# Attention in a three-stage kernel: the product with V from split float32r, batch by batch, to plain float32, both batches in column halves of one product

## The chip, the cores and the metric

The kernel runs on one core of a Trainium2 chip. The metric is the device time of one launch in microseconds (us). TensorE (PE) does the matrix products, and its weight loads are listed apart as PEld. VectorE is DVE, ScalarE is ACT, GpSimd is POOL, and SP issues most DMAs. TensorE and the transposes write to PSUM, and DVE or ACT move the results from there to SBUF.

## The reference, cut to what matters

```python
# attention: B, H, S, D = 4, 8, 576, 64
scores = scale * np.matmul(q, k.transpose(0, 1, 3, 2))
...
scores = scores + bias.transpose(2, 0, 1)[None, :, :, :]   # bias: a small MLP of the relative position
scores = scores - np.max(scores, axis=-1, keepdims=True)
attn = np.exp(scores)
attn = attn / (np.sum(attn, axis=-1, keepdims=True) + 1e-09)
return np.matmul(attn, v).astype(np.float32)
...
x = np.ascontiguousarray(attn_out.transpose(0, 2, 1, 3)).reshape(B * S, H * D)
x = _moe_ref(x=x, **moe_kwargs)          # router logits x @ w_gate, top expert of 8, two layers
return _moe2_ref(x=x, **moe2_kwargs)     # dense 512 -> 2048 -> 512
```

## The kernel before

The launch runs four phases one after the other: the position bias (`bias_phase`, to 78 us in the trace), attention (to 380 us), the experts (`moe1`) and the dense layers (`moe2`). Most products use the type float32r: a value is split into an upper part that float32r holds exactly and a lower rest, and three or two products of parts stand for one float32 product.

Attention goes through 32 units. A unit is (p, g, h): a pair p of batches (0 and 1, or 2 and 3), a group g of query rows (g = 0: rows 0 to 255, g = 1: rows 256 to 575) and a head h. The order is p, then g, then h, so there are four groups of eight units: (p, g) = (0,0), (0,1), (1,0), (1,1). A unit of g = 0 has four tiles of 128 query rows, two for each batch. One of g = 1 has five: the first takes 64 rows of either batch (`b` is None), then two for each batch.

Tile s goes through these stages, in steps of a software pipeline that is written out by hand, since PE, DVE, ACT and SP keep the order in which the code is written:

- step s: `stage_s` (scores, L429, into a PSUM tile `s` with two buffers), `stage_softmax` (L440 on DVE adds the bias and takes the row minimum of the negated scores, and a read of the accumulator follows), and late in the step `stage_exp` (L450 on ACT, with the row sum by an accumulator read).
- step s + 2: `stage_t` and `stage_r` transpose the 576 columns in four pieces of 128 (L463) and one of 64 (L473). `stage_hi` copies the upper part to `eh` on ACT (L487, L481; the 64-row rest L486, L479), and `stage_lo` subtracts on DVE to get the lower part `el` (L494, L507; the rest L499, L503).
- `AVL` = 4 steps after the last tile of a batch: `stage_av`, nine products (five with `eh` at L525, four with `el` at L527) whose weights are `vs`: V's upper part in 64 columns and its lower part in 64 more. `stage_oevac` copies the sums to `ot` on ACT (L538). So each unit has two such steps.
- one step later: `stage_j` (L549) multiplies `ot` by `jw`, 64 columns of identity (which adds the two parts of V) and 8 of the router's weights, and `stage_x` (L578, DVE) divides by the row sums into `xrow`. In g = 1 the 64-row rest has two more small products, L552 and L554, in the two column halves of TensorE's array.

`o` and `jp` share one PSUM buffer (`ps_v`). The scores' PSUM tile has two, so the scores of tile s + 2 wait until the exp of tile s has read its buffer:

```python
self.ps_s = eb.enter_context(tc.tile_pool(name="ps_s", bufs=2, space=PSUM))
self.ps_v = eb.enter_context(tc.tile_pool(name="ps_v", bufs=1, space=PSUM))
```

`load_kv` brings K and V of one batch and head into a raw buffer, and `prep_kv` splits both into `ks` and `vs`: casts on DVE or ACT (L321, L326, L324), subtractions on POOL (L322, L327). Twelve of the 32 are split in the bias phase, the rest within attention (`KVJ`, `KVR`, `KVA`), most of those of the second pair in group (0,1). Routing work of finished groups is fed in between, an operation or so a step (`slip`). At the end, `moe1` has the first expert's weights loaded by POOL into four buffers `stg`, whose space attention used before.

Of the kernel before, what the change touches and what calls it, by code (L numbers as in the profile page):

```python
# [120 lines left out]
def host_arrays(i):  # L121
# [21 lines left out]
    jw = np.zeros((2, 64, H, 72), np.float32)  # L143
    wg = i["moe_w_gate"].reshape(H, D, E).transpose(1, 0, 2)
    jw[:, :, :, 0:64] = np.eye(64, dtype=np.float32)[None, :, None, :]
    jw[:, :, :, 64:72] = wg[None]
    a["jw"] = jw.reshape(128, H, 72)
# [17 lines left out]
class Kernel:  # L165
# [4 lines left out]
    def bias_phase(self, prep_hook):  # L170
        nc, tc, a = self.nc, self.tc, self.a
        with ExitStack() as es:
# [11 lines left out]
            self.raw += [xp.tile([128, S + 5 * D], F32, name=f"kv{j}") for j in range(NRAW - 2)]  # L184
# [108 lines left out]
            PREP = 770.0 * KV0 / 26  # L293
# [12 lines left out]
    def load_kv(self, b, h):  # L306
        nc, a = self.nc, self.a
        bh = b * H + h
        buf = self.raw[self.nkv % len(self.raw)]
        self.nkv += 1  # L310
        kr, vr = buf[0:64, 0:S], buf[:, S:S + 5 * D].rearrange("p (c d) -> p c d", c=5)
# [4 lines left out]
    def prep_kv(self, b, h, veng):  # L316
        nc = self.nc
        kr, vr = self.kvraw.pop((b, h))
        vs = self.kv_p.tile([128, 5, 2 * D], F32R, tag="vs", name="vs")
# [56 lines left out]
    def attention(self):  # L376
# [4 lines left out]
        for u in units:  # L381
# [5 lines left out]
            for j, (bb, t) in enumerate(ts):  # L387
                tiles.append(dict(u=u, b=bb, t=t, c=4 if bb is None else 2 * bb + t, j=j, first=(j == 0), last=(j == len(ts) - 1),
                                  end=(bb is not None and t == 1)))
        n = len(tiles)  # L390
# [4 lines left out]
        def unit_state(u):  # L395
            if u not in st:
# [4 lines left out]
                d["eh"] = self.et_p.tile([128, 2, 5, 320], F32R, tag="eh", name="eh")  # L401
                d["el"] = self.et_p.tile([128, 2, 4, 320], F32R, tag="el", name="el")
                for bb in range(2):
                    d["eh", bb], d["el", bb] = d["eh"][:, 1 - bb], d["el"][:, 1 - bb]
# [70 lines left out]
        def stage_hi(i):  # L475
            T = tiles[i]
            d = st[T["u"]]
            if T["b"] is None:
                nc.scalar.activation(out=d["eh"][0:64, :, 4, 0:64], in_=d["rem", None].rearrange("p (b q) -> p b q", b=2),  # L479
                                     func=AF.Copy)  # L480
# [90 lines left out]
        def stage_x(i):  # L571
# [9 lines left out]
            if T["last"]:  # L581
# [9 lines left out]
                if h == H - 1:  # L591
                    self.routed.append((p, g))
# [1064 lines left out]
```

## Time and profile before

| | us |
|---|---|
| runs | 1093.06, 1093.54, 1095.12; median 1093.54 |
| the profiled execution | 1093.54, of which the span is 1091.9 |
| bias phase | to 78.06 |
| attention, group (0,0) / (0,1) / (1,0) | 58.67 / 90.88 / 64.81 |
| attention, group (1,1), to the end of its last full unit of work | 82.30 |
| from there to the end | 717 |

The groups are cut where the first L440 of a group starts, the last one 10.2 us after its last unit's first L440. "Busy" counts the time in which at least one instruction of an engine runs. Instructions of one engine overlap by some 0.08 us on DVE and ACT and by far more on PE, so the distance between starts, not the listed duration, is what an instruction costs its engine.

### The profile page before, as it was taken

The numbers are of one execution on the slowest core, as the hardware profiler recorded it, in microseconds if no ns is written. First come the engines' busy times: TensorE is split into PE (matmuls) and PEld (weight loads), VectorE is DVE, ScalarE is ACT, GpSimd is POOL, SyncE is SP. The second block draws the span as 40 slices with busy tenths as digits, with TensorE's granted clock in tenths as the row PEclk, the third lists the DMA queues.
The fourth block names the chain that finished last, engine by engine and source line by source line (L and its number), as shares of the span: only waits on it lengthen the run. The fifth ranks groups of instructions, "written<-read, shape, count | busy, mean of one in ns | idle before, by whom it ended". The sixth has DMA issues, their size and how long they took to land. (4 is left out here: it accounts for less than half of the span.)

```text
span 1091.9 us, 19524 instructions
## 1 busy us (share of the span) xinstructions
PE 1035.2 (95%) x6878; PEld 906.6 (83%) x6878; DVE 702.0 (64%) x1438; ACT 551.5 (51%) x1163; POOL 276.7 (25%) x437
## 2 busy tenths in 40 slices
PE   9999998999999989899899999999999999999996
PEld 3349988889998878777787888998989989899895
DVE  7779989989999895887887712533525335253350
ACT  7779877778787733444545513432424224242240
POOL 5646536665335343111211200000000000000000
PEclk9999999999999989999999999999999999999999
DMA  9985585764656477896744824600010100100000
GB/s 230 313 249 172 157 213 154 200 163 147 191 139 173 136 161 242 251 266 211 244 164 134 280 68 165 248 36 30 11 39 3 38 30 11 39 1 20 10 11 20
DMA packets 94566, 146.58 MB, mean 134 GB/s; under 512 B 11264, under 2 KB 53328, under 8 KB 94352
## 3 DMA queue, kind: packets, MB, share of 16 engines
q1 hardware_dynamic: 88976, 127.26, 39.8%
q0 software_dynamic: 5456, 17.70, 5.3%
q8 instruction: 64, 1.05, 0.4%
q14 instruction: 70, 0.57, 0.2%
HBM read 105.36 MB, written 36.70 MB: 130 GB/s over the span
## 5 line engine op out<-in xcount | busy, mean ns | idle before, releaser
L1415 PE MATMUL l1x<-xTl,wih 128*128 128x256 f32 x576 | 163.0, 283 | 0.0
L1415 PE MATMUL l1x<-xTh,wil 128*128 128x256 f32 x576 | 163.0, 283 | 0.0
L1415 PE MATMUL l1x<-xTh,wih 128*128 128x256 f32 x576 | 163.0, 283 | 0.0
L1423 DVE SCALAR_TENSOR_TENSOR t<-e,t 128x512 f32<-128x512 f32 x72 | 49.8, 692 | 132.8 <-ACT t L1422 132.8
L450 ACT ACTIVATE e<-s,mn 128x576 f32<-128x576 f32 x144 | 106.1, 737 | 33.1 <-DVE mn L440 26.8
L1439 POOL DMA_INDIRECT out<-y,idc x18 | 17.6, 979 | 395.2 <-ACT xTh L1404 271.3
L440 DVE CUSTOM_DVE_ANT_0 s<-s,bt 128x576 f32<-128x576 f32 x144 | 108.7, 755 | 7.3 <-PE s L429 4.3
L1434 PE MATMUL l2x<-woh,gTh 128*128 128x512 f32 x288 | 112.8, 392 | 0.0
L1434 PE MATMUL l2x<-wol,gTh 128*128 128x512 f32 x288 | 112.3, 390 | 0.0
L1434 PE MATMUL l2x<-woh,gTl 128*128 128x512 f32 x288 | 112.1, 389 | 0.0
L1415 PEld LDWEIGHTS l1x<-xTl,wih 128*128 128x128 f32 x576 | 110.6, 192 | 0.4
L1415 PEld LDWEIGHTS l1x<-xTh,wih 128*128 128x128 f32 x576 | 110.6, 192 | 0.4
L1415 PEld LDWEIGHTS l1x<-xTh,wil 128*128 128x128 f32 x576 | 110.6, 192 | 0.0
L1426 ACT ACTIVATE gTh<-t 128x512 fp32r<-128x512 f32 x72 | 45.5, 632 | 111.9 <-DVE t L1424 111.9
L429 PE MATMUL s<-ks,qh 128*128 128x288 f32 x320 | 92.7, 320 | 4.5 <-ACT e L450 4.4
L494 DVE TENSOR_TENSOR el<-t,eh 128x512 fp32r<-128x512 f32 x128 | 87.4, 683 | 2.8 <-DMA xgat<-in_kT 0.7
L463 PE MATMUL t<-ident,e 128*128 128x128 f32 x576 | 86.8, 273 | 0.5 <-DVE el L494 0.5
L1438 ACT ACTIVATE y<-l2x 128x512 f32<-128x512 f32 x18 | 10.8, 598 | 142.6 <-PE l2x L1434 142.6
L1427 DVE TENSOR_TENSOR gTl<-t,gTh 128x512 fp32r<-128x512 f32 x72 | 49.8, 692 | 50.4 <-ACT gTh L1426 50.4
L1188 PE MATMUL l2m<-w2h,hTl 128*128 128x512 f32 x168 | 69.9, 416 | 10.1 <-DVE hTl L1147 10.1
L487 ACT ACTIVATE eh<-t 128x512 fp32r<-128x512 f32 x128 | 75.2, 588 | 5.8 <-PE t L463 4.2
L1188 PE MATMUL l2m<-w2h,hTh 128*128 128x512 f32 x168 | 70.5, 419 | 5.8 <-ACT hTh L1146 5.6
(248 smaller groups left out, 2510.5 us busy)
## 6 DMA issues: line engine op xcount, KB each, us to landing
bt<-bias SPq DMA_DIRECT2D x32, 576.0 KB, 5.0
stg<-in_moe_w SPq DMA_DIRECT2D x32, 512.0 KB, 4.2
dec_w<-in_w SPq DMA_DIRECT2D x32, 512.0 KB, 5.4
bias<-o SPq DMA_DIRECT2D x36, 295.5 KB, 5.0
x_d<-y SPq DMA_DIRECT2D x22, 260.0 KB, 4.1
qraw<-in_qT SPq DMA_DIRECT2D x32, 160.0 KB, 3.7
k<-ks SPq DMA_DIRECT2D x32, 144.0 KB, 4.2
bt<-bias SPq DMA_DIRECT2D x32, 144.0 KB, 5.9
```

The costliest lines, as they stand in the source:

```text
L429: nc.tensor.matmul(out=ps[:, half, 0:288], lhsT=x, rhs=k[:, half * 288:half * 288 + 288], start=(m == 0), stop=(m == len(seq) - 1))
L440: nc.vector.tensor_tensor_reduce(out=sc, in0=sc, in1=bt[:, t, :].rearrange("p (a k) -> p a k", a=2), scale=-0.125, scalar=3.0e38, op0=ALU. ...
L450: nc.scalar.activation(out=e.rearrange("p (a k) -> p a k", a=2), in_=T["ps"][:, :, 0:288], func=AF.Exp, scale=-1.0, bias=T["mn"], accum_ou ...
L463: nc.tensor.transpose(out=tp[:, c, :], in_=e[:, 128 * c:128 * c + 128], identity=ident)
L487: nc.scalar.activation(out=d["eh", T["b"]][:, 0:4, o:o + 128], in_=T["tp"], func=AF.Copy)
L494: nc.vector.tensor_tensor(out=d["el", bb][:, 0:4, o:o + n_], in0=src, in1=d["eh", bb][:, 0:4, o:o + n_].bitcast(F32), op=ALU.subtract)
L1188: nc.tensor.matmul(out=p, lhsT=hT[h][:, k, 128 * t:128 * t + 128], rhs=w2[wt][:, k, :], start=(k == 0 and h == wt), stop=(k == 7 and wt == 1))
L1415: nc.tensor.matmul(out=p[:, m, :], lhsT=wi[wt][:, k, ms], rhs=xT[x][:, k, :], start=(n == 0), stop=(n == 11))
L1423: V.scalar_tensor_tensor(out=t, in0=e, scalar=1.0, in1=t, op0=ALU.add, op1=ALU.mult)
L1426: nc.scalar.activation(out=gT[0][:, gs, :], in_=t, func=AF.Copy)
L1427: V.tensor_tensor(out=gT[1][:, gs, :], in0=t, in1=gT[0][:, gs, :].bitcast(F32), op=ALU.subtract)
L1434: nc.tensor.matmul(out=p, lhsT=gT[h][:, k, 128 * t:128 * t + 128], rhs=wo[wt][:, k, :], start=(n == 0), stop=(n == 47))
```

## The change

V is no longer split: `load_kv` brings it straight into `vs` (plain float32, 20 buffers), and `prep_kv` handles K alone. The transposed weights are not split either: `stage_hi` and `stage_lo` become `stage_e`, one copy to a float32 tile `et`, on ACT for the four big pieces and on DVE for the 64-row rest. The two `et` tiles are fixed, used by units in turn, and rows 64 to 127 of their fifth piece are set to zero once. `stage_av` runs once a unit, four steps after its last tile: five pieces, each with one product for either batch in its own column half (64 weights columns, `tile_position`), in plain float32. `stage_oevac` is one copy on DVE instead of two on ACT. `stage_j` has two products of 144 columns instead of four of 72, since `jw` now has a block for each half, and `stage_x` is one operation a unit. Special orders for the last tiles (`late`, `tail_psum`) are gone. `PREP`, the load that the bias phase's planner books on DVE for the preparation of K and V, falls from 770 to 350 per unit of it.

```diff
-    jw = np.zeros((2, 64, H, 72), np.float32)
+    jw = np.zeros((2, 64, H, 2, 72), np.float32)
...
-            PREP = 770.0 * KV0 / 26
+            PREP = 350.0 * KV0 / 26
...
+        vs = self.kv_p.tile([128, 5, D], F32, tag="vs", name="vs", bufs=20)
         nc.sync.dma_start(out=kr, in_=a["kT"][bh])
-        nc.sync.dma_start(out=vr, in_=a["v"][bh])
-        self.kvraw[b, h] = (kr, vr)
...
+        nc.sync.dma_start(out=vs, in_=a["v"][bh])
+        self.kvraw[b, h] = (kr, vs)
...
-        if veng == "a":
-            nc.scalar.activation(out=vs[:, :, 0:D], in_=vr, func=AF.Copy)
-        else:
-            nc.vector.tensor_copy(out=vs[:, :, 0:D], in_=vr)
-        nc.gpsimd.tensor_tensor(out=vs[:, :, D:2 * D], in0=vr, in1=vs[:, :, 0:D].bitcast(F32), op=ALU.subtract)
...
+        for j in range(2):
+            et = self.et_p.tile([128, 2, 5, 320], F32, name=f"et{j}")
+            nc.gpsimd.memset(et[64:128, :, 4, :], 0.0)
+            ets.append(et)
...
-            if T["end"]:
-                nc.scalar.activation(out=d["eh", T["b"]][0:64, 4, o - 128:o + 128], in_=d["rem", T["b"]], func=AF.Copy)
-            nc.scalar.activation(out=d["eh", T["b"]][:, 0:4, o:o + 128], in_=T["tp"], func=AF.Copy)
-
-        def stage_lo(i):
+            if T["end"]:
+                nc.vector.tensor_copy(out=d["et", T["b"]][0:64, 4, o - 128:o + 128], in_=d["rem", T["b"]])
+            nc.scalar.activation(out=d["et", T["b"]][:, 0:4, o:o + 128], in_=T["tp"], func=AF.Copy)
+
+        def stage_av(i):
...
             for c in range(5):
-                nc.tensor.matmul(out=o[:, :N], lhsT=vs[:, c, :], rhs=eh[:, c, :N], start=(c == 0), stop=False)
-            for c in range(4):
-                nc.tensor.matmul(out=o[:, :N], lhsT=vs[:, c, :], rhs=el[:, c, :N], start=False, stop=(c == 3))
+                for bb in range(2):
+                    nc.tensor.matmul(out=o[64 * bb:64 * bb + 64, :N], lhsT=self.kv[2 * p + bb, h][1][:, c, :],
+                                     rhs=d["et", bb][:, c, :N], start=(c == 0), stop=(c == 4),
+                                     tile_position=(0, 64 * bb))
             T["o"] = o
...
+            d["ot"] = self.o_p.tile([128, 320], F32, tag="ot", name="ot")
+            nc.vector.tensor_copy(out=d["ot"][:, :N], in_=T["o"][:, :N])
...
+            jp = ps_v.tile([128, 5, 72], F32, tag="v", name="jp")
             for t in range(2):
-                nc.tensor.matmul(out=jp[:, t, :], lhsT=d["ot", bb][:, o0 + 128 * t:o0 + 128 * t + 128],
-                                 rhs=jw[:, h, :], start=True, stop=True)
...
+                nc.tensor.matmul(out=jp[:, t:4:2, :], lhsT=d["ot"][:, o0 + 128 * t:o0 + 128 * t + 128],
+                                 rhs=jw[:, h], start=True, stop=True)
...
-        av_at = {i + AVL: i for i, T in enumerate(tiles) if T["end"]}
+        av_at = {i + AVL: i for i, T in enumerate(tiles) if T["last"]}
```

On TensorE, in a unit of group (0,0), this stands before; the names are the PSUM tiles of the stages (`s` scores, `t` and `r` transposes, `o` the product with V, `jp` the last product).

```order
L463 MATMUL t<-ident,e 128x128 x4
L473 MATMUL r<-ident,e 64x128
L525 MATMUL o<-eh,vs 128x256 x5
L527 MATMUL o<-el,vs 128x256 x4
L429 MATMUL s<-ks,qh_194 128x288
L429 MATMUL s<-ks,ql_195 128x288
L429 MATMUL s<-ks,qh_194 128x288
L429 MATMUL s<-ks,ql_195 128x288
L463 MATMUL t<-ident,e 128x128 x4
L473 MATMUL r<-ident,e 64x128
L549 MATMUL jp<-jw,ot 128x72 x2
```

And this stands at the same place in the changed kernel, where four score and transpose steps follow each other for one such block.

```order
L463 MATMUL t<-ident,e 128x128 x4
L473 MATMUL r<-ident,e 64x128
L497 MATMUL o<-et_985,vs 64x256 x10
L429 MATMUL s<-ks,qh_200 128x288
L429 MATMUL s<-ks,ql_201 128x288
L429 MATMUL s<-ks,qh_200 128x288
L429 MATMUL s<-ks,ql_201 128x288
L463 MATMUL t<-ident,e 128x128 x4
L473 MATMUL r<-ident,e 64x128
L516 MATMUL jp<-jw,ot 128x2x72 x2
```

The block of nine that stood in every second step is now one of ten half-wide products in every fourth, and the two steps between no longer hold anything but scores and transposes.

On DVE, over two tiles of the same group, this stands before (the two rows L440 are the softmax operation and the read of its accumulator).

```order
L440 ISA s,mn<-s,bt 128x2x288
L440 ISA mn 128x1
L569 RECIPROCAL ri<-ri 128x2
L499 TENSOR_TENSOR eh<-r,eh 64x256
L494 TENSOR_TENSOR el<-t,eh 128x4x128
L440 ISA s,mn<-s,bt 128x2x288
L440 ISA mn 128x1
L578 TENSOR_TENSOR xrow<-jp,ri 128x2x72
L494 TENSOR_TENSOR el<-t,eh 128x4x128
```

In the changed kernel it is this, at the step with the product and the one after it.

```order
L440 ISA s,mn<-s,bt 128x2x288
L440 ISA mn 128x1
L531 RECIPROCAL ri<-ri 128x4
L485 COPY et_983<-r 64x256
L507 COPY ot<-o 128x256
L440 ISA s,mn<-s,bt 128x2x288
L440 ISA mn 128x1
L539 TENSOR_TENSOR xrow<-jp,ri 128x4x72
```

The subtractions are gone, and the copy of `o`, which ACT held, now stands ahead of the next tile's L440.

## Rows read from the trace of the kernel before

**Rows 1.** The page: span, busy time and instructions of each engine.

```profile
span 1091.9 us, 19524 instructions
...
PE 1035.2 (95%) x6878; PEld 906.6 (83%) x6878; DVE 702.0 (64%) x1438; ACT 551.5 (51%) x1163; POOL 276.7 (25%) x437
```

**Rows 2.** Busy time in windows, the four attention groups in turn.

```profile
core 0: us, PE busy (x) PEld busy (x) DVE busy (x) ACT busy (x) POOL busy (x), PEclk, DMA share, GB/s
78.06:136.73 58.67, 56.34 (x468) 55.40 (x467) 54.21 (x141) 50.78 (x128) 31.44 (x52) 1.00 0.58 169
136.73:227.61 90.88, 82.37 (x638) 77.27 (x636) 84.21 (x222) 67.16 (x174) 54.94 (x82) 1.00 0.74 190
227.61:292.42 64.81, 60.96 (x490) 59.17 (x491) 62.30 (x176) 52.04 (x133) 34.70 (x58) 0.97 0.56 161
292.42:374.72 82.30, 79.40 (x626) 75.15 (x625) 76.57 (x219) 62.92 (x162) 30.31 (x65) 1.00 0.53 145
```

**Rows 3.** Timeline of PE, half a unit of group (0,0): start, duration, line.

```profile
99.19 0.56 PE L549 MATMUL jp<-jw,ot 128*128 128x72 f32 x4
99.55 0.38 PE L429 MATMUL s<-ks,qh 128*128 128x288 f32 x1
...
100.17 0.60 PE L463 MATMUL t<-ident,e 128*128 128x128 f32 x4
...
100.63 0.84 PE L525 MATMUL o<-eh,vs 128*128 128x256 f32 x5
...
101.78 0.30 PE L429 MATMUL s<-ks,qh 128*128 128x288 f32 x1
...
102.32 0.60 PE L463 MATMUL t<-ident,e 128*128 128x128 f32 x4
...
102.86 0.56 PE L549 MATMUL jp<-jw,ot 128*128 128x72 f32 x4
103.23 0.38 PE L429 MATMUL s<-ks,qh 128*128 128x288 f32 x1
```

**Rows 4.** Timeline of PE in the bias phase; L269 is plain float32 in column quarters.

```profile
9.89 1.06 PE L269 MATMUL l<-h,w 128*32 128x512 f32 x8
10.89 1.20 PE L247 MATMUL l<-xt,wr 128*128 128x512 f32 x4
```

**Rows 5.** The same L269 products by windows: pieces that run in each.

```profile
core 0: us, PE busy (x), PEclk, DMA share, GB/s
9.92:10.33 0.41, 0.41 (x4) 1.00 1.23 204
10.33:10.37 0.04, 0.04 (x8) 1.00 1.09 154
```

**Rows 6.** Timeline of PEld, weight loads of the same products.

```profile
9.89 0.16 PEld L269 LDWEIGHTS l<-h,w 128*32 128x32 f32 x8 [0.37 <-issue]
```

**Rows 7.** Timeline of PE, group (0,1): the rest's products in column halves.

```profile
154.08 0.28 PE L552 MATMUL jp<-jw,ot 128*64 128x72 f32 x1
154.09 0.28 PE L554 MATMUL jp<-jw,ot 128*64 128x72 f32 x1
...
154.36 0.40 PE L429 MATMUL s<-ks,qh 128*128 128x288 f32 x1
```

**Rows 8.** Line L552: weight loads, min, median and max ns.

```profile
L552 PEld LDWEIGHTS jp<-jw,ot x32: 132/134/137, 154.1 to 380.4; 128*64 128x64 f32 x32
```

**Rows 9.** Timeline, one tile's scores and softmax, another's exp.

```profile
371.90 0.29 PE L429 MATMUL s<-ks,qh 128*128 128x288 f32 x1
...
372.63 0.77 DVE L440 CUSTOM_DVE_ANT_0 s<-s,bt 128x576 f32<-128x576 f32 x1 [0.24 <-PE s L429]
...
373.31 0.14 DVE L440 DVE_READ_ACCUMULATOR2_ANT mn<- 128x1 f32 x1
...
100.26 0.74 ACT L450 ACTIVATE e<-s,mn 128x576 f32<-128x576 f32 x1 [0.36 <-DVE mn L440]
100.90 0.19 ACT L450 ACTIVATION_READ_ACCUMULATOR e<-s,mn 128x1 f32 x1
```

**Rows 10.** DVE by line and shape, group (0,1).

```profile
L494 DVE TENSOR_TENSOR el<-t,eh 128x512 fp32r<-128x512 f32 x32 | 21.8, 680 | 0.5
L321 DVE CAST ks<-xgat 64x576 fp32r<-64x576 f32 x8 | 6.8, 846 | 0.0
L499 DVE TENSOR_TENSOR eh<-r,eh 64x256 fp32r<-64x256 f32 x16 | 6.7, 418 | 0.5
L507 DVE TENSOR_TENSOR el<-t,eh 128x512 fp32r<-128x512 f32 x8 | 5.5, 692 | 0.3
```

**Rows 11.** Timeline around the end of attention: PE, DVE and POOL.

```profile
376.06 0.97 PE L525 MATMUL o<-eh,vs 128*128 128x320 f32 x5
...
377.45 0.90 PE L525 MATMUL o<-eh,vs 128*128 128x320 f32 x5
...
378.97 0.49 DVE L536 COPY ot<-o 128x320 f32<-128x320 f32 x1 [0.76 <-PE o L527]
...
375.36 3.11 POOL L1093 DMA_DIRECT2D stg<-in_moe_w  x4 [0.76 <-issue]
```

**Rows 12.** Bias phase: a wait of ACT, and the load of `jw` (page, KB).

```profile
47.69 0.30 ACT L261 ACTIVATE o<-l 128x160 f32<-128x160 f32 x1 [2.44 <-DMA bias<-o]
...
jw<-in_jw SPq DMA_DIRECT2D x1, 288.0 KB
```

More of the change, by code (lines that the diff above doesn't have):

```diff
@@ L183, in bias_phase @@
             xg = list(self.raw)
-            self.raw += [xp.tile([128, S + 5 * D], F32, name=f"kv{j}") for j in range(NRAW - 2)]
+            self.raw += [xp.tile([128, S], F32, name=f"kv{j}") for j in range(NRAW - 2)]
             xb = [xp.tile([128, 1024], F32R, name=f"xt{j}") for j in range(4)]
@@ L389, in attention @@
                                   end=(bb is not None and t == 1)))
+        ets = []
+        for j in range(2):
+            et = self.et_p.tile([128, 2, 5, 320], F32, name=f"et{j}")
+            nc.gpsimd.memset(et[64:128, :, 4, :], 0.0)
+            ets.append(et)
         n = len(tiles)
@@ L551, in stage_j @@
-            if g == 1 and bb == 1:
-                nc.tensor.matmul(out=jp[0:64, 2, :], lhsT=d["ot", 1][:, 0:64], rhs=jw[:, h, :], start=True, stop=True,
-                                 tile_position=(0, 0))
-                nc.tensor.matmul(out=jp[64:128, 2, :], lhsT=d["ot", 0][:, 0:64], rhs=jw[:, h, :], start=True,
-                                 stop=True, tile_position=(0, 64))
+                nc.tensor.matmul(out=jp[:, t:4:2, :], lhsT=d["ot"][:, o0 + 128 * t:o0 + 128 * t + 128],
+                                 rhs=jw[:, h], start=True, stop=True)
@@ L556, in stage_j @@
+            if g == 1:
+                for j in range(2):
+                    nc.tensor.matmul(out=jp[64 * j:64 * j + 64, 4, :], lhsT=d["ot"][:, 0:64], rhs=jw[:, h, 1 - j],
+                                     start=True, stop=True, tile_position=(0, 64 * j))
             T["jp"] = jp
-        def sums(T):
-            return slice(2, 4 + T["u"][1]) if T["b"] else slice(0, 2)
         def stage_ri(i, k):
             T = tiles[i]
-            d, c = st[T["u"]], sums(T)
+            d, w = st[T["u"]], 4 + T["u"][1]
@@ L593, in stage_x @@
+            if h < H - 1:
+                acc, part = self.lacc[:, :w], xr[:, :w, D * (h + 1):D * (h + 1) + 8]
+                if h == 0:
+                    nc.gpsimd.tensor_copy(out=acc, in_=part)
+                else:
+                    nc.gpsimd.tensor_tensor(out=acc, in0=acc, in1=part, op=ALU.add)
+            else:
+                self.routed.append((p, g))
             if h in (H - 3, H - 1):
                 c0, c1 = (0, D * (H - 2)) if h < H - 1 else (D * (H - 2), DM)
-                places = self.x_places(p, g, c0, c1)
@@ L596, in stage_x @@
-                for dst, src in places[2 * bb:2 * bb + 2] + (places[4:] if bb == 1 else []):
+                for dst, src in self.x_places(p, g, c0, c1):
                     nc.sync.dma_start(out=dst, in_=src(xr)[:, c0:c1])
@@ L621, in attention @@
                 stage_r(s - 2)
-                stage_hi(s - 2)
-            late = s - 2 in av_at and s == n + AVL - 1
-            if s - 1 in av_at and s != n + AVL - 2:
+                stage_e(s - 2)
+            if s - 1 in av_at:
                 stage_j(av_at[s - 1])
@@ L1479, in build @@
                 self.rr_p = ea.enter_context(tc.tile_pool(name="rr", bufs=1))
-                self.jw = self.rr_p.tile([128, H, 72], F32, name="jw")
+                self.jw = self.rr_p.tile([128, H, 2, 72], F32, name="jw")
                 self.raw_p = ea.enter_context(tc.tile_pool(name="raw", bufs=3))
@@ L1595, in build @@
                         self.lacc = self.xr_p.tile([128, 5, 8], F32, name="lacc")
[L1596 removed]
+                        self.raw.append(self.xr_p.tile([128, S], F32, name="raw"))
                         self.ohs = self.xr_p.tile([128, 5 * (128 + 2 * NCOL)], BF16, name="ohs")
```

105 lines of the change are left out of this document (25 added, 80 removed).

## Prediction

> **What bounds the kernel now.** I read the page first: PE is busy for 1035.2 of 1091.9 us [rows 1], but a share over four phases with different limits decides nothing here. The change touches attention, so I cut attention into its four groups [rows 2]. The reader is to see that they have two limits. In (0,0) eight units take 58.67 us, 7.33 each, with PE busy for 56.34 and DVE for 54.21. In (0,1) a unit takes 11.36, and DVE, busy for 84.21 of 90.88 us, is ahead of PE (82.37): it also splits most of the second pair's K there and does the routing of the first group. (1,0) takes 8.10 a unit with DVE ahead again, and (1,1) 10.29 with PE ahead a little. The timeline of PE in (0,0) then shows half a unit without any gap [rows 3]: the last products `jp` start at 99.19, scores at 99.55, transposes at 100.17, the product with V at 100.63, scores at 101.78, transposes at 102.32, `jp` at 102.86. From `jp` to `jp` is 3.67 us, and twice that, 7.34, is a unit: where nothing disturbs, PE's own work sets the pace. DVE has 88% of its own beside it.
>
> **What TensorE pays and gets.** A score block of an ordinary tile costs 0.54 us (101.78 to 102.32) and a transposed tile with its rest 0.54 (102.32 to 102.86), or 0.46 where the product with V follows [rows 3]. That product costs 1.15 in g = 0 (100.63 to 101.78) and 1.39 in g = 1 (376.06 to 377.45) [rows 3, 11], twice a unit: 2.30 and 2.78.
>
> The new product is plain float32, which the trace has in the bias phase. L269 has four products of 512 columns there, one for each quarter of the array's columns, and each is recorded as two pieces. From 9.89 to 10.89, 1.00 us, all eight pass [rows 4]; one after the other at 0.6 us each they would need almost 5. The windows show how: four run until 10.33, and the second four have started by 10.37 [rows 5]. So parts of the array in different columns stream at the same time, each from its own data, and a round of 512 columns takes 0.44 to 0.48 us, 0.86 to 0.94 ns a column. In two halves instead of quarters the trace has L552 and L554, which start 0.01 us apart [rows 7]. I take 0.89 ns. The new block is five pieces of V by two rounds: 10 x 256 columns x 0.89 = 2.28 us in g = 0, 10 x 320 x 0.89 = 2.85 in g = 1, and some 0.07 for the change of layout behind it (1.00 us less two rounds of 0.46 in rows 4 leaves 0.08). That is 2.35 and 2.92 (2.25 to 2.5 and 2.8 to 3.1 by the bounds) against 2.30 and 2.78. **The product itself gets no cheaper.** A column costs 2 x 0.89 = 1.78 ns in float32 against 1.15 / 9 / 256 = 0.50 in float32r; two batches side by side, and five products for each instead of nine, give just that back.
>
> A rule speaks against more than that. All ten rounds use all 128 rows, and between two rounds new weights are loaded; L552's load of 64 columns takes 134 ns [rows 8]. In L269 all eight loads are over by 10.05 [rows 4, 6], while the first round runs until 10.33 [rows 5]: the second round's weights were loaded under the first. The Trainium skill, "TensorE: Matmul & The Clock Gate", section "Part 3: Packing small matmuls — row/col tiling", says that weight loads overlap running products only where the row groups differ. By that rule nothing would be hidden here; the trace does not agree. Its result is a rival below.
>
> `jp` becomes two products of 144 columns, four pieces of 144 x 0.89 = 0.13, 0.51 in all, some 0.60 with the start of the next scores, against 2 x 0.36 (99.19 to 99.55) before. In g = 1 the rest adds 0.28 (154.08 to 154.36 [rows 7]) as before.
>
> **Where a unit's time goes then.** DVE loses the subtractions. In (0,1) these are 21.8 + 5.5 + 6.7 us in the rows shown and 2.3 for the smaller rest, 36 in all [rows 10]; it gets the copies of the rest from ACT (24 of some 0.3) and eight copies of `o` at 0.49 [rows 11], so its 84 us fall to about 60. ACT loses the copies of `o` and of the rest, and POOL and ACT the splitting of V. No engine but PE is then near its limit, and the next limit is a chain. Scores of tile s + 2 wait for the exp of tile s. From the start of the scores to the softmax is 0.73 us (371.90 to 372.63), to the end of its read 0.82 (372.63 to 373.45), to exp 0.09 (100.17 to 100.26), to the end of exp's read 0.83 (to 101.09) [rows 9]: 2.47, and about 0.08 for the next start, 2.55. Before, every pair of steps held a product with V or `jp`, and PE had more than 2.55 us of other work. Now one pair of steps in a unit has neither: 4 x 0.54 = 2.16.
>
> I walk through a unit of g = 0 from the end of a product with V. Scores at 0, transposes, `jp`, scores at 1.68, scores at 2.76; the next would start at 3.84 by PE, but the exp of the tile at 1.68 is through at 1.68 + 2.55 = 4.23. Then scores and transposes until 5.31, and the product until 7.66. So 7.65 us against 7.34 without disturbance, 0.38 of them a wait. In g = 1 the first scores take 0.80: the second tile starts at 1.34, the third at 2.82 (its chain, for PE alone 2.42), the fourth at 3.90, the product runs from 4.98 to 7.90, and scores, transposes and `jp` (0.88) bring the unit to 9.86. I take 9.85.
>
> **The sum**, by groups, against [rows 2]:
> - (0,0): 8 x 7.65 = 61.2, +2.5.
> - (0,1): 8 x 9.85 = 78.8, and 2.5 for casts of K (0.846 us [rows 10]) and routing that stand ahead of a score's softmax on DVE. This 2.5 is a choice between 0 and the 9 us of all twelve casts; most fall in gaps now. 81.3, -9.6.
> - (1,0): 61.2 + 1.5 in the same way, -2.1.
> - (1,1): 78.8 + 1.5, -2.0.
> - Bias phase: DVE's relief is hidden, since PE runs there without a gap but for one wait on the DMA of finished rows [rows 12]. `jw` is 288 KB larger, about 1 us at some 300 GB/s of that stretch, and makes that wait longer: +1 (0 to 1.5).
> - End of attention: one product of 2.92 us replaces the last two of 1.39, a stall on `el` goes, `o` is copied once: 0. The POOL loads of `stg` started at 375.36, before the last products [rows 11]; in the new order three of the four stand behind the last product. Their results were needed 5 to 10 us later, so I take 0 (to +2).
>
> That is -10.2 us. The experts and dense layers start from routing and weights that come after attention, so they move along. The profiled execution took 1093.54, which is also the median: **1083.3 us**.
>
> **Rivals.**
> - *The chain is longer than I read it* (slower). On DVE the copy of `o` waits for the product, and the next tile's softmax stands behind it; ACT's copies stand ahead of exp. At 2.9 us instead of 2.55 a unit of g = 0 takes about 8.1 and one of g = 1 about 10.2: 16 x (0.45 + 0.35) = +12.8, 1096. It decides from 0.32 us a unit on (10.2 / 32). For it: the exact fit of four steps. Against it: DVE is idle for a quarter of the time then.
> - *PE alone sets the pace* (faster): no wait in either walk, 7.27 and 9.46; 16 x (0.38 + 0.39) = -12.3, 1071. For it: 7.34 before was PE alone, with DVE far fuller.
> - *Given back*: DVE's gaps in (0,1) were not its limit but waits for POOL, DMA and PSUM, which stay, or the later `stg` delays the first expert: 5 to 9 us back, about 1092, no change.
> - *Halves do not overlap as quarters do*: the product takes 4.6 and 5.8 us, 16 x (2.3 + 2.9) = +83, 1166. Rows 7 speak against it.
> - *Weight loads exposed* (the rule above): ten rounds x 0.134 = 1.34 us in each unit, 32 x 1.34 = +43, 1126.
>
> **How the numbers follow.** Forecast 0.55 (1078 to 1089), chain 0.16, PE alone 0.13, given back 0.10, the last two 0.06 together. 0.2% is 2.2 us here, about what a measurement can tell. Faster: 0.55 + 0.13 = 0.68. Within 0.2%: given back, and a little of the chain, 0.12. Slower: 0.20. The range goes from PE alone to the chain's value, 1070 to 1096; outside stay the last two rivals and part of the chain's.
>
> **What would show it.** The product with V at 2.3 and 2.9 us from its first piece to the next scores, two halves starting together; units of (0,0) at 7.6 to 7.7 with one wait of PE for ACT's exp ahead of the fourth scores; (0,1) near 10.2 a unit with DVE at about 75%; the experts' phase as long as before. I am wrong if (0,0) gains, if the product takes over 2.6 us, or if (0,1) stays above 10.8.

## The result, and the profile after

The changed kernel takes 1107.45 us (median of four runs, 1103.14 to 1112.76) against 1093.3 us of the kernel before on the same chip: a ratio of 1.013, interval 1.0082 to 1.0178. I had predicted 1083.3 us, in 1070 to 1096. It became slower, outside the range and on the other side. The profiled execution is the slowest of the four.

The first two rows of its page [rows 1 answer to them]: DVE's work fell by 86 us, PE's rose by 11.

```profile
span 1110.8 us, 18872 instructions
...
PE 1046.3 (94%) x6814; PEld 863.7 (78%) x6814; DVE 615.6 (55%) x1256; ACT 506.8 (46%) x993; POOL 242.4 (22%) x375
```

The windows of the four attention groups (columns as in [rows 2]; the fourth runs here to the last `jp`), then the stretch from the last `jp` to the dense layers' first product `l1x`:

```profile
76.90:137.20 60.30, 57.15 (x447) 46.26 (x446) 37.71 (x103) 41.14 (x94) 26.45 (x42) 1.00 0.64 166
137.20:229.80 92.60, 83.63 (x620) 64.86 (x618) 59.77 (x175) 54.17 (x122) 41.79 (x62) 0.98 0.73 185
229.80:295.00 65.20, 62.61 (x477) 49.26 (x478) 44.45 (x135) 42.33 (x96) 28.85 (x45) 0.97 0.62 162
295.00:392.20 97.20, 89.89 (x657) 68.24 (x654) 55.13 (x176) 54.41 (x123) 30.69 (x60) 0.96 0.48 127
392.20:692.00 299.80, 268.98 (x1584) 231.63 (x1583) 202.06 (x353) 121.54 (x191) 60.36 (x91) 0.95 0.64 195
```

The kernel before in the same two last windows:

```profile
292.40:380.50 88.10, 84.63 (x666) 80.12 (x667) 80.19 (x229) 65.94 (x167) 33.67 (x71) 1.00 0.54 148
380.50:672.60 292.10, 266.12 (x1583) 230.23 (x1584) 203.13 (x353) 120.55 (x190) 57.82 (x88) 0.96 0.64 198
```

In the second group DVE needs 59.8 us instead of 84.2, as forecast, and the group still takes 92.6 instead of 90.9. The fourth takes 97.2 instead of 88.1, the last window 299.8 instead of 292.1. Where DVE was the fullest engine it has become idle, and nothing was gained: it waits now.

PE's timeline in the middle of (0,0), one unit from score to score [rows 3 answer to it]:

```profile
101.08 0.40 PE L429 MATMUL s<-ks,qh 128*128 128x288 f32 x1 [0.24 <-ACT e L450]
...
101.72 0.60 PE L463 MATMUL t<-ident,e 128*128 128x128 f32 x4
102.15 0.27 PE L473 MATMUL r<-ident,e 128*64 128x128 f32 x1
102.36 2.38 PE L497 MATMUL o<-et,vs 128*64 128x256 f32 x20
104.67 0.40 PE L429 MATMUL s<-ks,qh 128*128 128x288 f32 x1
...
105.85 0.66 PE L516 MATMUL jp<-jw,ot 128*128 128x144 f32 x4
106.25 0.39 PE L429 MATMUL s<-ks,qh 128*128 128x288 f32 x1
...
108.93 0.40 PE L429 MATMUL s<-ks,qh 128*128 128x288 f32 x1 [0.24 <-ACT e L450]
```

The product with V is what I took it for: 2.31 us (102.36 to 104.67). The unit is 7.85 us, score at 101.08 to score at 108.93, with one short wait of PE for exp. But see a tile without anything else: 104.67 to 105.85, 1.18 us, where I had 1.08.

Then the place where the fourth group begins. DVE, POOL and PE there, one view each:

```profile
296.03 0.46 DVE L539 TENSOR_TENSOR xrow<-jp,ri 128x288 f32<-128x288 f32 x1 [0.17 <-issue]
299.48 0.19 DVE L688 TENSOR_TENSOR y<-lacc,mb 128x32 f32<-128x32 f32 x1 [2.99 <-POOL lacc L548]
...
300.15 0.76 DVE L440 CUSTOM_DVE_ANT_0 s<-s,bt 128x576 f32<-128x576 f32 x1
```

```profile
298.04 0.29 POOL L357 CAST qh<-qraw 128x128 fp32r<-128x128 f32 x1 [4.77 <-DMA qraw<-in_qT]
298.42 0.70 POOL L360 TENSOR_TENSOR qx<-qraw,qh 64x64 fp32r<-64x64 f32 x2
299.19 0.25 POOL L548 TENSOR_TENSOR lacc<-lacc,xrow 128x32 f32<-128x32 f32 x1
```

```profile
298.75 0.60 PE L463 MATMUL t<-ident,e 128*128 128x128 f32 x4
301.29 0.40 PE L473 MATMUL r<-ident,e 128*64 128x128 f32 x1 [1.94 <-DVE et L485]
301.88 0.61 PE L429 MATMUL s<-ks,qh 128*128 128x288 f32 x1 [0.19 <-ACT e L450]
...
303.00 1.05 PE L463 MATMUL t<-ident,e 128*128 128x128 f32 x4
303.85 0.42 PE L473 MATMUL r<-ident,e 128*64 128x128 f32 x1
```

Read it backwards. PE waits for a copy of DVE, DVE stood 2.99 us in front of L688, a routing operation of 0.19 us, which waits for `lacc`. POOL could have added it from 296.5 on (`xrow` at 296.03 plus 0.46), but in its order a cast of q stands ahead, and that one waits for a load until 298.04. In the kernel before POOL had the two the other way round at this place:

```profile
293.48 0.25 POOL L590 TENSOR_TENSOR lacc<-lacc,xrow 128x32 f32<-128x32 f32 x1 [1.17 <-DVE xrow L578]
296.56 0.29 POOL L361 CAST qh<-qraw 128x128 fp32r<-128x128 f32 x1 [2.83 <-DMA qraw<-in_qT]
```

That engines run strictly in their own order is also what the Trainium skill, "Perfetto Trace Analysis", section "Tensor Engine Instruction (MATMUL, LD_WEIGHTS)", says of ACT, DVE and GPSIMD; these rows agree.

Why the loads come late shows in SP's queue some microseconds on, with the softmax and the cast that wait for them:

```profile
309.20 1.76 SPq L554 DMA_DIRECT2D x_d<-xrow  x4
311.06 1.12 SPq L368 DMA_DIRECT2D k<-ks  x2
312.27 1.03 SPq L332 DMA_DIRECT2D qraw<-in_qT  x2
313.35 0.43 SPq L340 DMA_DIRECT2D bt<-bias  x1
```

```profile
322.23 0.77 DVE L440 CUSTOM_DVE_ANT_0 s<-s,bt 128x576 f32<-128x576 f32 x1 [2.87 <-DMA bt<-bias]
```

```profile
318.29 0.29 POOL L357 CAST qh<-qraw 128x128 fp32r<-128x128 f32 x1 [8.48 <-DMA qraw<-in_qT]
```

The four transfers of finished rows wait for `xrow` (308.73), and K, q and the bias of the next units are issued only behind them. Over all of attention DVE waits (line waited for: us in total, times, longest) in the changed kernel and in the kernel before:

```profile
DVE y L688 <- POOL lacc L548: 8.4, 3, 3.3
DVE s L440 <- DMA bt<-bias: 5.9, 2, 3.1
```

```profile
DVE y L737 <- POOL lacc L590: 2.4, 1, 2.4
DVE s L440 <- DMA bt<-bias: 1.0, 1, 1.0
```

The end of attention [rows 11 answer to it], POOL:

```profile
387.86 0.84 POOL L1038 DMA_DIRECT2D stg<-in_moe_w  x1
391.09 2.26 POOL L1038 DMA_DIRECT2D stg<-in_moe_w  x3 [2.39 <-PE o L497]
```

Three of the four first loads of `stg` wait for the last product with V, and the last is issued by 1.17 us after the last `jp` (392.18); before, all four were issued by 2.05 us ahead of it. PE's longest wait behind it (2.8 us in a second profile of the same kernel):

```profile
PE l L1087 <- DVE w1l L1053: 4.1, 1, 4.1
```

Theory, then: late small steps at the group changes (lacc's place on POOL, rows ahead of loads on SP) and late `stg` loads, on top of a unit that I summed too short. Rival: the lump of the product itself, which leaves the chain from scores to exp uncovered.

### The profile page after: what moved, and what is told of

Same layout as the page of the kernel before. It is cut to its first block, busy times and chain, and to the rows that moved or that the text cites. A ratio compares the mean times of both kernels' runs of the same rounds, so it can differ in the third digit from the quotient of the medians.

```text
span 1110.8 us, 18872 instructions
## 1 busy us (share of the span) xinstructions
PE 1046.3 (94%) x6814; PEld 863.7 (78%) x6814; DVE 615.6 (55%) x1256; ACT 506.8 (46%) x993; POOL 242.4 (22%) x375
## 5 line engine op out<-in xcount | busy, mean ns | idle before, releaser
L440 DVE CUSTOM_DVE_ANT_0 s<-s,bt 128x576 f32<-128x576 f32 x144 | 109.9, 765 | 44.0 <-PE s L429 31.1
L486 ACT ACTIVATE et<-t 128x512 f32<-128x512 f32 x128 | 76.2, 595 | 101.9 <-PE t L463 99.2
L429 PE MATMUL s<-ks,qh 128*128 128x288 f32 x320 | 100.7, 344 | 17.6 <-ACT e L450 17.2
L450 ACT ACTIVATE e<-s,mn 128x576 f32<-128x576 f32 x144 | 106.8, 742 | 15.9 <-DVE mn L440 9.7
L429 PEld LDWEIGHTS s<-ks,qh 128*128 128x128 f32 x320 | 58.7, 190 | 44.4 <-ACT e L450 25.9
L497 PE MATMUL o<-et,vs 128*64 128x320 f32 (+1 forms) x640 | 87.2, 418 | 0.0
```

Of the source, the lines that this page charges most:

```text
L429: nc.tensor.matmul(out=ps[:, half, 0:288], lhsT=x, rhs=k[:, half * 288:half * 288 + 288], start=(m == 0), stop=(m == len(seq) - 1))
L440: nc.vector.tensor_tensor_reduce(out=sc, in0=sc, in1=bt[:, t, :].rearrange("p (a k) -> p a k", a=2), scale=-0.125, scalar=3.0e38, op0=ALU. ...
L450: nc.scalar.activation(out=e.rearrange("p (a k) -> p a k", a=2), in_=T["ps"][:, :, 0:288], func=AF.Exp, scale=-1.0, bias=T["mn"], accum_ou ...
L486: nc.scalar.activation(out=d["et", T["b"]][:, 0:4, o:o + 128], in_=T["tp"], func=AF.Copy)
L497: nc.tensor.matmul(out=o[64 * bb:64 * bb + 64, :N], lhsT=self.kv[2 * p + bb, h][1][:, c, :], rhs=d["et", bb][:, c, :N], start=(c == 0), st ...
```

## The experiments

One table for all runs, in us: median and ratio to the kernel before on the same chip with its 95% interval; the groups (0,0), (0,1), (1,0), and (1,1) to its last `jp`, attention as their sum, and "phase" from there to the first `l1x`, all from starts in each run's profile.

```
run           median   ratio  interval          (0,0) (0,1) (1,0) (1,1)  attention  phase
before        1093.3                             58.7  90.9  64.8  88.1    302.5    292.1
changed       1107.45  1.0130 1.0082 to 1.0178   60.3  92.6  65.3  97.2    315.3    299.8
e8_same       1106.36  1.0113 1.0059 to 1.0167   60.3  88.8  64.8  96.6    310.5    298.3
e1_lacc       1099.27  1.0067 1.0040 to 1.0095   60.2  86.5  65.0  93.3    305.0    294.2
e2_rows       1096.49  1.0032 1.0008 to 1.0055   60.2  85.8  65.1  90.1    301.2    300.5
e3_vmem       1100.13  1.0066 1.0039 to 1.0093   60.2  92.4  65.2  93.1    310.9    294.2
e4_three      1091.09  0.9976 0.9955 to 0.9997   60.2  84.7  63.6  90.1    298.6    295.1
e5_split      1095.24  1.0013 0.9990 to 1.0037   58.5  85.3  63.0  91.5    298.3    300.8
e6_four       1090.40  0.9978 0.9960 to 0.9996   58.5  83.3  62.9  90.8    295.6    297.4
e7_prep       1108.43  1.0130 1.0091 to 1.0169   60.3  92.3  66.7  93.8    312.9    298.3
b1_rows       1087.88  0.9936 0.9919 to 0.9952   57.9  89.4  63.4  89.4    300.0    289.5
e9_leave      1051.95  0.9612 0.9594 to 0.9630   54.3  78.0  57.4  80.8    270.5    281.1
e10_split0    1089.17  0.9948 0.9929 to 0.9966   58.5  85.4  62.1  91.1    297.1    296.5
e11_last      1089.82  0.9957 0.9937 to 0.9978   58.6  85.4  62.1  90.8    296.9    293.8
e12_norows    1086.56  0.9928 0.9904 to 0.9951   58.5  85.4  62.1  90.8    296.8    292.5
```

**The changed kernel again**, beside e4, e6 and e7. 

> The changed kernel itself, once more and beside the other versions. Theory: 1104 to 1110 us as the first time, with the experts' phase near 299.8 us. Rival (part of the first time was chance: where half-clock stretches fell): 1099 to 1103 us.

 It took 1106.36 us: the loss stands. Between the two profiles single units differ by up to 1.6 us, so single units are compared with care below.

**lacc's last addition on DVE.**

```diff
-                    nc.gpsimd.tensor_tensor(out=acc, in0=acc, in1=part, op=ALU.add)
+                    (nc.vector if h == H - 2 else nc.gpsimd).tensor_tensor(out=acc, in0=acc, in1=part, op=ALU.add)
```

> The last addition to lacc of each group runs on DVE instead of POOL, where it stands behind the casts of q that wait for a load. Theory (late small steps at the change of a group stop DVE's queue, and with it softmax, exp and PE): DVE's 8.4 us of idle time ahead of L688 fall below 1 us, and a half-clock stretch or two behind them go; 1099 to 1103 us against 1107.45 of the changed kernel. Rival (another late thing, the rows of bias or q, stops the same steps at nearly the same time): 1106 to 1109 us.

 1099.27 us. The waits in front of L688 are gone from DVE's list, and the first unit of the fourth group, 14.5 us in the changed kernel, takes 11.0. The two units behind it stay at 12.4 and 11.8: another cause is left there.

**Rows behind the loads.**

```diff
-                for dst, src in self.x_places(p, g, c0, c1):
-                    nc.sync.dma_start(out=dst, in_=src(xr)[:, c0:c1])
+                rows_out.extend((dst, src(xr)[:, c0:c1]) for dst, src in self.x_places(p, g, c0, c1))
...
                 self.unit_hook(uidx[T["u"]], T["j"])
+                while T["j"] == 0 and rows_out:
+                    dst, x = rows_out.pop(0)
+                    nc.sync.dma_start(out=dst, in_=x)
...
```

> The transfers of finished rows (x_d<-xrow) are issued behind the next unit's loads on SP instead of ahead of them. Theory (loads that stand behind these rows on SP come late in the first units of g = 1): the waits of softmax for bt (3.1 us in the second group, 2.9 in the fourth) and most of POOL's wait for qraw go, 3 to 7 us less: 1101 to 1105 us. Rival (lacc's stop and the copies on DVE set these units anyway): 1106 to 1109 us.

 1096.49 us, more than I had expected. The waits for `bt` are gone, and those for `lacc`, whose place on POOL did not change, fell too. DVE's list of waits in attention has left of them

```profile
DVE y L694 <- POOL lacc L548: 3.1, 3, 2.2
```

against 8.4 us. So the cast that stands ahead of `lacc` was late because its load stood behind the rows: one cause, two waits. The first three units of the fourth group are 11.0, 10.4 and 10.7 us, those of the second 10.1, 10.4 and 10.4.

**V behind K in memory.**

```diff
                 self.kv_p = ea.enter_context(tc.tile_pool(name="kv", bufs=16))
+                self.v_p = ea.enter_context(tc.tile_pool(name="v", bufs=20))
...
-        vs = self.kv_p.tile([128, 5, D], F32, tag="vs", name="vs", bufs=20)
+        vs = self.v_p.tile([128, 5, D], F32, tag="vs", name="vs")
```

> V's 20 buffers lie behind K's in memory, so that no stg buffer lies where the last heads' V is read. Theory (three of the four first loads of stg wait for the last product with V, and the experts' first slot starts late by that): the four loads start some 3 us earlier against the end of attention, and the stretch from the last jp to the first l1x falls from 299.8 to 296 or 297 us; 1103 to 1105.5 us in all. Rival (the first slot is late because of routing and clock, not the loads): that stretch stays within 1 us of 299.8, 1106 to 1109 us.

 POOL issues the four loads in one go, ahead of the last `jp` (387.72):

```profile
383.24 3.09 POOL L1038 DMA_DIRECT2D stg<-in_moe_w  x4 [0.74 <-PE r L473]
```

The stretch to `l1x` falls to 294.2, 5.6 us less than in the first profile of the changed kernel and 4.1 less than in the second, more than expected; attention, 310.9, stays as in the second profile. 1100.13 us. The length of that stretch alone would not prove the cause: in e1, where V lies as in the changed kernel, it is 294.2 too, with less half clock in it (0.97 of the full clock over the stretch, 0.95 in both profiles of the changed kernel). What e3 alone shows is the wait itself: the last split `w1l` of the first loads starts 8.9 us after the last `jp`, against 13.5 and 15.9 in the changed kernel and 12.5 in e1, and PE's wait for it, 4.1 and 2.8 us there and 3.1 in e1, is gone.

**The product in two parts.**

```diff
-            if T["j"] == 0 and T["u"][1] == 1 or T["j"] == 2 and T["u"][1] == 0:
+            if T["j"] == 2:
...
-            if s - 1 in av_at:
-                stage_j(av_at[s - 1])
-                stage_x(av_at[s - 1])
+            if s - 2 in av_at:
+                stage_j(av_at[s - 2])
+                stage_x(av_at[s - 2])
             if s in av_at:
-                stage_av(av_at[s])
-                stage_oevac(av_at[s])
+                stage_av(av_at[s], range(0, 3))
+            if s - 1 in av_at:
+                stage_av(av_at[s - 1], range(3, 5))
+                stage_oevac(av_at[s - 1])
```

> The product with V of a unit in two parts, blocks 0 to 2 in one step and 3 and 4 in the next, jp one step later; the routing's PSUM steps at the third tile in both kinds of units. Theory (one lump of 2.3 to 2.9 us leaves a pair of steps with nothing but scores and transposes, and the chain from scores to exp is longer than that): units of (0,0) fall from 7.85 to 7.3 to 7.5, those of g = 1 from 10.36 to 9.7 to 9.9, 1092 to 1100 us with the late steps at the group changes still there. Rival (every step waits for ACT or DVE, whatever PE holds): units stay within 0.1 us, 1105 to 1110 us.

 1095.24 us, in the range, but not for the reason: steady units of g = 0 go from 7.85 only to 7.70, those of g = 1 from 10.36 up to 10.5. (The run also moves the routing's PSUM steps in g = 1 to the third tile.) The unit in PE's timeline, now without any wait:

```profile
102.94 1.52 PE L499 MATMUL o<-et,vs 128*64 128x256 f32 x12
104.39 0.40 PE L429 MATMUL s<-ks,qh 128*128 128x288 f32 x1
...
105.65 1.08 PE L499 MATMUL o<-et,vs 128*64 128x256 f32 x8
106.67 0.40 PE L429 MATMUL s<-ks,qh 128*128 128x288 f32 x1
...
107.86 0.66 PE L517 MATMUL jp<-jw,ot 128*128 128x144 f32 x4
108.26 0.39 PE L429 MATMUL s<-ks,qh 128*128 128x288 f32 x1
```

The two parts cost 1.45 and 1.02, 0.16 more than the lump. Another 0.16 goes into the transposes and scores around them, since two tiles now have a part of the product behind their transposes and not one. Against that stands the wait for exp: in the changed kernel the scores at 108.93 start 0.51 behind the last transpose (108.42), where 0.04 is usual (107.31 to 107.35), so it costs 0.47. The split pays 0.32 for 0.47, and with no wait at all the unit is 7.70: most of a unit is PE's own work. The gain in attention lies in the first three units of the groups of g = 1 and in the last unit of (0,1) (13.31 to 10.24), and SP's queue has a reason for it: `jp` one step later puts the rows of a group's last unit behind the next loads, as e2 did on purpose (in this run K, q and bias are issued from 287.12 to 296.1 and the rows at 297.67). That link was not tried apart from the split.

**The three small edits together, and all four.** 

> All three small edits together: lacc's last addition on DVE, finished rows behind the next loads, V behind K in memory. Theory (the loss has two places, the first units of g = 1 and the first loads of stg; attention then takes about 300.5 us as with the rows alone, or a little less, and the experts' phase about 294): 1087 to 1091 us, ahead of the kernel before. Rival (the gains come from the same few microseconds and do not add): 1094 to 1097 us.

 1091.09 us, at the edge of the expected range and ahead of the kernel before by 0.24% (0.03 to 0.45). Attention is 298.6, somewhat better than expected. By the ratios the three edits alone are worth 5, 9 and 5 us against e8, and together 15: they share a part. 

> The three small edits and the product with V in two parts. The split alone saved attention 17 us, of which only 0.14 us a unit in steady units of g = 0 (7.70 against 7.84) and nothing in those of g = 1 (10.5 against 10.36), so most of it lay in the first units of a group. Theory: it then adds little where the rows are already out of the way, attention 298 to 301 us, 1085 to 1090 us. Rival (both gains add): attention below 296 us, 1080 to 1084 us.

 1090.40 us: attention falls to 295.6, as the rival had it, but the experts' phase gives 2.4 us back, and the total lies in neither expected range and cannot be told from that of e4. Windows of e4, second and fourth group:

```profile
136.20:221.00 84.80, 81.97 (x620) 63.83 (x618) 61.61 (x177) 54.14 (x122) 41.00 (x59) 1.00 0.84 198
284.60:374.60 90.00, 86.53 (x654) 66.14 (x654) 55.66 (x178) 54.83 (x124) 31.12 (x60) 1.00 0.57 140
```

PE is busy for 97% and 96% of them now, 90% and 92% in the changed kernel: with the late steps gone the groups are PE's.

**The planner's charge in the bias phase.**

```diff
-            PREP = 350.0 * KV0 / 26
+            PREP = 770.0 * KV0 / 26
```

> The changed kernel with the planner's charge for the K and V work in the bias phase back at 770. The bias phase ended 1.2 to 1.6 us earlier after the change, where I had expected 1 us later. Theory (the better split of the copies between ACT and DVE gave that): first softmax 1 to 2 us later than in the changed kernel. Rival (less work on POOL, ACT and DVE gave it, whatever the charge): first softmax within 0.4 us of it.

 The first softmax starts at 80.74 us, against 76.90 and 77.29 in the two profiles of the changed kernel: later, and by more than the theory said. But a granted clock of 0.52 from 49.7 to 56.5 belongs to that: 6.8 us that hold 3.5 us of full clock, so 3.3 us of the difference. The changed kernel's first profile has a half as long stretch there, its second none. And in b1 (below), the old form with its charge of 770 and with no such stretch, the first softmax starts at 76.67. Neither sign nor size of an effect of the charge is shown.

**The same edits in the kernel before** (rows behind the loads, lacc's last addition on DVE). 

> The kernel before the change with two of the small edits: finished rows behind the next unit's loads, lacc's last addition of a group on DVE. It prices what the kernel before itself loses there. Theory (the late small steps are the new order's doing; before, softmax waited 1.0 us for bt and DVE 2.4 us for lacc): 0 to 3 us less than before, 1090 to 1093.5 us. Rival (both kernels lose the same there, and the edits say nothing on the change): 8 us less or more, 1085 us or below.

 1087.88 us, 6.5 less than the kernel before in the same runs: between theory and rival, and by its median the fastest version that computes everything. So the same edits are worth 6.5 us to the old form, where the three edits took 15 off the new one. Where these 6.5 us come from is not shown: between the two profiles attention is shorter by only 2.5 us, with (1,1) longer by 1.3, and 1.4 us lie in the bias phase, which the edits do not touch and where the kernel before has a half-clock stretch. The new form with its edits (e10, 1089.17, in the same runs) is not ahead of the old form with its own; the intervals of the two ratios overlap.

**Two of five blocks of V left out**, on e4.

```diff
-            for c in range(5):
+            for c in (0, 1, 4):
```

> The three small edits, and two of the five blocks of V left out of the product (so the weighted sums lack 256 of 576 keys). Theory (in an undisturbed unit TensorE's own work sets the pace, and my sum of it was too short): 4 of 10 rounds go, 0.92 us of 2.31 and 1.14 of 2.84; units of (0,0) fall from 7.84 to 6.9 to 7.1 and those of (1,1) from 10.36 to 9.2 to 9.4. Rival (the chain from scores to exp sets the pace): units fall by less than 0.4 us.

 Steady units fall from 7.84 to 6.99 and from 10.36 to 9.26, by 0.85 and 1.10 where the rounds left out are worth 0.92 and 1.14. So the rounds of the product count almost in full, and no chain from scores to exp covers them: but for one wait, TensorE's own work sets the pace in an undisturbed unit. That wait for exp stays as it was (0.23 us of idle time ahead of the scores at 105.62). (The rest of that run's gain is no guide: its routing sees other numbers, and its experts' phase is 14 us shorter.)

**Two parts in g = 0 alone**, on e4. 

> The three small edits, and the product in two parts only in units of g = 0, where the parts gained 0.14 us a unit. Theory: 2 us less than with the three edits alone (1091.09), 1088 to 1090 us, about 4 us ahead of the kernel before. Rival (what is gained in attention goes into the experts' first slot): 1090 to 1092 us.

 1089.17 us, 0.5% ahead of the kernel before, as the theory had it; attention 297.1, but the experts' phase is 296.5.

**What still holds up the first expert.** In e4, e6 and e10 the phase is 3 to 5 us longer than in the kernel before. Two runs, both on e10. In the first the last six transfers of rows go out from ACT's queue:

```diff
-                nc.sync.dma_start(out=dst, in_=x)
+                (nc.scalar if len(rows_out) < 6 else nc.sync).dma_start(out=dst, in_=x)
```

> The three small edits, the product in two parts in units of g = 0, and the very last six transfers of finished rows issued from ACT's queue instead of SP's, where they stand right ahead of the second loads of stg. With the three edits these loads still started 4.95 us after the last jp (3.73 before the change) and ACT's last copy of them 20.8 us after it (17.6 before). Theory (the six transfers at once, a product of the joint rows, hold up the first slot): the loads start 2.5 to 4 us after the last jp, the stretch from the last jp to the first l1x falls from 296.5 to 292 to 294 us, 1085 to 1087.5 us in all. Rival (the first slot is late through DVE's work and the clock): that stretch stays within 1 us, 1088 to 1090.5 us.

 1089.82 us, no gain. The second loads of `stg` started 7.55 us after the last `jp`, not earlier: ACT now issued the rows ahead of its own copies of the first loads. So the run says nothing on the theory, though its phase, 293.8 us, is as short as the theory had it. In the second they are left out (`if len(rows_out) >= 6` ahead of the issue). 

> The version with the product in two parts in g = 0, and the very last six transfers of finished rows left out (the last head of the last group never reaches the experts). Before the change two of the six left 0.74 us ahead of the last jp and the second loads of stg started 3.73 us after it; with the joint rows all six leave 0.83 us after it and the loads start 4.92 us after it. Theory (the six rows on SP hold the second loads up): the loads start 2.5 to 4 us after the last jp and ACT's last copy of them ends 2 to 4 us earlier (it starts 20.95 us after it now). Rival (the loads wait for the splits of the first ones, which start late): the loads start at 4.5 us or later, as now.

 The loads start at 4.13 us after the last `jp`, only 0.8 earlier, between the two answers. What moves more is when they are there. ACT's copies `w2h` in e10 (last `jp` at 373.40) and in e12 (373.57):

```profile
387.17 1.05 ACT L1061 ACTIVATE w2h<-stg 128x1024 fp32r<-128x1024 f32 x1
...
394.34 1.06 ACT L1061 ACTIVATE w2h<-stg 128x1024 fp32r<-128x1024 f32 x1 [2.96 <-DMA stg<-in_moe_w]
```

```profile
383.96 2.00 ACT L1062 ACTIVATE w2h<-stg 128x1024 fp32r<-128x1024 f32 x2
...
388.42 1.06 ACT L1062 ACTIVATE w2h<-stg 128x1024 fp32r<-128x1024 f32 x1 [0.18 <-DMA stg<-in_moe_w]
```

The first copy starts 3.4 us earlier after the last `jp` (10.39 against 13.77), the last 6.1: without the rows in front of them the second loads land sooner. The phase is 292.5 instead of 296.5, but that this comes from the loads is not shown: e11's is 293.8 with the first copy later than in e10 (16.03), and the intervals of the total ratios of e10 and e12 overlap. A part of that phase's length is where half-clock stretches fall, which no run here controls.

## Why the prediction was wrong

**Right.** The product with V: 2.31 and 2.84 us (370.33 to 373.17 in the fourth group), forecast 2.35 and 2.92. The halves overlap and the weight loads are hidden: ten exposed loads of 0.134 us would have made 3.7 us of it. The Trainium skill, "TensorE: Matmul & The Clock Gate", section "Part 3: Packing small matmuls — row/col tiling", says in its list of what overlaps that loads overlap running products only where the row groups differ, though the same section also has loads run ahead into a background weight buffer; these rows do not agree with the list. DVE's relief in (0,1), to 59.8 us where I wrote about 60. A loss in (0,0), 1.6 us of the 2.5, but that the two are so near is luck: the undisturbed unit takes 7.85 and not 7.65, eight of which would be 62.8, and the group's first unit takes 5.50 (6.89 before), since no product of this group falls into it; the sum had neither.

**The step that failed first: the two groups of g = 1.** I gave them 2.5 and 1.5 us for casts of K and for routing, since "most fall in gaps now", and put the wait for POOL, DMA and PSUM into a rival of 0.10. I costed what DVE has to do and not when its inputs come. The joint product makes one `xrow` of two, so that the first batch's rows no longer leave early; and POOL's order, which the code does not write out, put `lacc` behind the casts of q. POOL and SP, both served in order, turn this into late q, late bias and a stopped DVE. The forecast was -9.6 and -2.0; the profile has +1.7 and +9.1. With the three small edits the second group falls from 92.6 to 84.7 and the fourth from 97.2 to 90.1: 15 us of lateness (11 by the second profile of the changed kernel), 5.1 of which (1.7 in the second profile) are the half-clock stretches behind the waits, told of below. (1,0) has the same in small: +0.4 where I forecast -2.1, with one wait of PE of 3.5 us at 231.59.

**The second: the end of attention, "0 (to +2)".** It cost 7.7 us by the first profile, 6.2 by the second. I had seen that three `stg` loads stand behind the last product and trusted that "their results were needed 5 to 10 us later". They were not that far off: PE waited 4.1 us for the split of these weights. e3 took that wait away, and its phase is 4 to 6 us shorter, a part of which can be the clock (e1). For the rest the cause stays open: the rows that now leave all at once ahead of the second loads make these land later (e12), and the clock counts too.

**A mis-sized term: scores and transposes, 1.08 us a tile.** I took 0.54 for a score block from the one behind the old product with V (101.78 to 102.32); the other one in [rows 3], behind `jp`, takes 0.62 (99.55 to 100.17), and I passed over it. In the new order every score block stands behind transposes, `jp` or the new product, none behind a float32r product with V, and takes 0.62 to 0.64 (101.08 to 101.72): its first product lasts 0.40 us there, 0.30 at 101.78 in the kernel before. And a transposed tile takes 0.64 where the new product follows (101.72 to 102.36), 0.46 where the old one did (100.17 to 100.63). Why the first one behind such a change takes longer was not tried. So an ordinary tile costs 1.10 to 1.28. An undisturbed unit of g = 1 is 10.36 instead of 9.85, one of g = 0 7.85 instead of 7.65; the half microsecond on sixteen units is 8 us. In g = 0 the four tiles cost 0.35 more than in my walk, the wait for exp 0.47 instead of 0.38, and `jp` 0.40 (105.85 to 106.25) instead of 0.60, which hid half of it. This closes the account of e4: forecast for attention -11.2, measured -3.8 (298.6 against 302.5), and the difference of 7.4 lies in the two groups of g = 1 (84.7 against 81.3, and 2.0 more than before where 2.0 less were forecast). The wait for exp that I had walked to is there, 0.09 us above its forecast in g = 0 and 0.13 in g = 1 (0.53 instead of 0.40, ahead of the scores at 318.43 in e4). In g = 1 the tiles, and not this wait, make most of the half microsecond.

**Bias phase, +1.** It ended 0.8 to 1.2 us earlier in the two profiles of the changed kernel, and neither that nor the microsecond for `jw` is shown to be the change's doing: b1, the old form, ends it at 76.67, and the runs of the new form without a half-clock stretch there at 76.0 to 77.8.

**DVE's share in an undisturbed unit of (0,0), "88%".** No row has it. [rows 2] gives 54.21 of 58.67 us, 92%, and from 99.19 to 106.53 DVE is busy for 7.21 of 7.34 us, so that PE was not the only full engine there.

The rival that came nearest by its number was "the chain is longer" (1096), with the wrong mechanism: a chain, but through POOL and SP and at the group changes, not in each unit. By mechanism it was "given back", waits for POOL and DMA and a later `stg`: it had both places, at 5 to 9 us where they cost over 20 together, and I gave it 0.10.

And the comparison itself deserves a word: b1 shows that the same edits are worth 6.5 us to the old form. Put against each other with their edits (b1 and e10), old form and new are equal within what these runs can tell.

## What to carry to other kernels

An engine that was relieved is worth only what its inputs allow: for each gap that a forecast fills, name what has to arrive there, on which in-order queue, and what stands ahead of it. When results of two parts are joined into one, list everything that was triggered by the earlier part (here two or three transfers of rows) and look for what stands behind these on their queues. Durations of a block hold for its neighbours: take them from a place with the neighbours that the new order has.

## What was not expected of the hardware

In the changed kernel's attention the granted clock falls to half (1.2 of 2.4 GHz) four times, before the change once. Two of the four stretches, by windows (PE's clock is the third column from the end):

```profile
301.30:304.70 3.40, 3.21 (x14) 2.32 (x16) 1.66 (x6) 2.34 (x7) 0.00 (x0) 0.51 0.02 5
325.20:328.60 3.40, 3.40 (x15) 2.46 (x15) 1.77 (x8) 2.61 (x7) 0.05 (x1) 0.51 0.12 31
```

Each of the four begins within 1.5 us after PE has stood still for 1.9 to 3.5 us (the row at 301.29 above is one of them); a wait of 1.90 at 142.16 was followed by none, and neither were the short ones in steady units. In the second profile there are two such stretches, and a wait of 2.26 at 321.21 was followed by none. While it lasts the work takes twice as long: four transposes take 0.85 us there (303.00 to 303.85) and 0.43 otherwise (101.72 to 102.15). In e4, where PE's longest wait in attention is 1.6 us, all windows of attention have 1.00. A late step costs its wait, and here often 1.7 us behind it (half of 3.4).
